# Moving weight loads, token loads and shifted-value loads earlier in a sliding-window attention plus gated feed-forward kernel

## The chip, the cores and the metric

The kernel runs on one core of one Trainium2 chip. The metric is device time in microseconds (us) of one execution. The engines are PE (TensorE, matrix multiplication), PEld (its weight loads), DVE (VectorE), ACT (ScalarE), POOL (GpSimd) and SP (SyncE, which here only issues DMAs). The DMAs that SP issues are in one hardware queue of the page, those that POOL issues in a software queue (when e4, below, gave POOL's 2.78 MB of weight loads to SP, the hardware queue's sum went from 38.48 to 41.26 MB and the software queue's from 13.46 to 10.67). The page counts the packets of both as shares of the same 16 DMA engines (50.8% and 14.2% in the kernel before).

For a kernel on one core, a run is called slow when it is over 1.5% above the fastest run of the same kernel, and fast otherwise. Ratios use fast runs alone.

## The reference, cut to what matters

```python
x  = A_x                                    # 1 x 2048 x 640, bf16
xn = layernorm(x)
# A: 32 heads of 20; a token attends to itself and 7 tokens before it, 2 apart
q, k, v = split(xn @ wqkv)
attn = softmax(q . k[t - 2w], w = 0..7)     # masked where t - 2w < 0
a = (sum_w attn[w] * v[t - 2w]) @ wo
# B: gated feed-forward, no nonlinearity
b = ((xn @ w_gate) * (xn @ w_up)) @ w_down  # 640 -> 1536 -> 640
out = x + a + b
```

## The kernel before: the parts that matter

The 2048 tokens are worked in four chunks of 512. For each chunk, PE makes q, k and v (`psqk`, `psv`), gate and up (`psg`, `psu`) and the output and down projections (`psf`). DVE multiplies q with eight shifted copies of k (the products `pw`); PE sums them per head (`lps`); ACT takes the exponential (`e`). The weights are then stored to memory (`eD`), loaded back transposed (`eT`) and normalised (`rs`), and DVE multiplies them with eight shifted copies of v (`v8`, called `v_606`, `v_729`, `v_855`, `v_929` or only `v` in the profiles) and adds them up. From the second chunk on the normalised tokens `xn` are also stored (`xnD`) and loaded back transposed (`xnT`), for PE to read.

Three pieces of code matter. First, the store and the transposing load of the tokens. The tile `xn` comes from the pool tag `pw`, which has six buffers:

```python
if ttl == 0:
    st["xn"] = apool.tile([P, CH, D], BF, name="xn", tag="pw", bufs=6)
# ...
def keep():
    nc.sync.dma_start(out=xnD[c*CS:(c+1)*CS, :].rearrange(...), in_=st["xn"][:])
    later.append((turn_all, lambda t=clock["dve"]: t + 4.0))
def turn_all():
    nc.sync.dma_start_transpose(out=st["xnT"][:], in_=xnD[...].rearrange(...))
```

Second, the products. They use the same six buffers, so the sixth product after a chunk's `xn` lands in the buffer from which that `xn` is being stored, and waits until the store has landed (4.9 us on the page of the changed kernel, below):

```python
def product(g=g, j=j):
    pt = apool.tile([P, KT, CS], BF, name="pw", tag="pw", bufs=6)
    nc.vector.tensor_tensor(pt[:], st["qT"][:], st["kT"][:, :, off:off+CS], ALU.mult)
```

Third, the loads of the output and down weights, on POOL, and the program's order:

```python
def load_down():
    for jl in range(JL):
        nc.gpsimd.dma_start(out=wo_perm[jl*H:(jl+1)*H, :, :], in_=wo_r[jl])
    nc.gpsimd.dma_start(out=wd[:], in_=B_w_down.rearrange("(f p) d -> p f d", p=P))
# ...
norm(0, 1)
side(load_ffn)                 # gate and up, on POOL
norm(1, 4)
side(constants)
later.append((lambda: load_x(2), when(("turned", 1))))
later.append((load_down, when(("xn", 2, CH - 1))))
weights(0)
side(lambda: want_v8(0))
later.append((lambda: want_v8(1), when(("turned e", 0))))
# ...
```

`side` and `later` feed a small scheduler in the kernel: it simulates PE and DVE while the program is built, and so decides in what order instructions and DMA issues are written.

The softmax here doesn't subtract the row's maximum and nothing guards it: scores larger than these inputs give would overflow.

Of the kernel before, what the change touches and what calls it, by code (L numbers as in the profile page):

```python
# [17 lines left out]
def kernel(  # L18
# [29 lines left out]
    CH = 4  # L48
# [29 lines left out]
    def tcols(ttl):  # L78
        return slice(ttl * P, (ttl + 1) * P)
# [13 lines left out]
    def load_x(c, ttls=range(CH)):  # L93
        for ttl in ttls:
            tg = c * CH + ttl
            x_t = cpool.tile([P, D], BF, name="x_t", bufs=6)
            nc.sync.dma_start(out=x_t[:], in_=x_flat[tg * P : (tg + 1) * P, :])
            x_tiles[tg] = x_t
# [65 lines left out]
    def warm_up(n):  # L164
        wps = ps_log.tile([P, CS], F32, name="wps", tag="lg")
        for k in range(n):
            nc.tensor.matmul(wps[:, 0:P], lhsT=warm[:], rhs=warm[:], start=True, stop=True)
# [5 lines left out]
    clock = {"pe": 5.0, "dve": 2.7, "act": 0.0, "pool": 4.0}  # L173
    main, chain = deque(), deque()
    burst, quick, later = [], [], []
    done = {}
    rings = {"mm": (5, []), "tr": (2, []), "lg": (1, []), "pw": (6, [])}

    def when(*names):
        return lambda: max((done.get(n, INF) for n in names), default=0.0)  # L180

    def on(eng, name, ready, took):
        clock[eng] = max(clock[eng], ready) + took
        done[name] = clock[eng] + LAG

    def op(queue, name, emit, took, need=None, after=None, ring=None, slack=0.0):
        def ready():
            t = need() + slack if need else 0.0
            if ring:
                n, users = rings[ring[0]]  # L190
                if len(users) >= n:
                    t = max(t, done.get(users[-n], INF))
            return t

        queue.append((name, emit, took, ready, after, ring))
# [30 lines left out]
    def norm(c, group):  # L226
        st = state[c]
        st["xnT"] = None

        def alloc():  # L230
            if st["xnT"] is None:
                st["xnT"] = cpool.tile([P, KT, CS], BF, name="xnT", bufs=3)

        def steps(t0):
            g = {}

            def stats():
                g["mv"] = cpool.tile([P, group, nc.vector.BN_AGGR_DIM], F32, name="mv", bufs=2)
                for k in range(group):
                    x_t = x_tiles[c * CH + t0 + k]  # L240
                    s = cpool.tile([P, 2, nc.vector.BN_STATS_DIM], F32, name="stats")
                    for hf in range(2):
                        nc.vector.bn_stats(s[:, hf, :], x_t[:, hf * N2 : (hf + 1) * N2])  # L243
                    nc.vector.bn_aggr(g["mv"][:, k, :], s[:])
                rstd = cpool.tile([P, group], F32, name="rstd", bufs=2)
                g["rstd"] = rstd
                if c == 0 and t0 < 2:
                    nc.scalar.activation(rstd[:], g["mv"][:, :, 1], ACT.Sqrt, bias=eps[:])
                    return
                nc.gpsimd.tensor_scalar(rstd[:], g["mv"][:, :, 1], EPS, None, op0=ALU.add)  # L250
                nc.gpsimd.tensor_tensor(
                    rstd[:], rstd[:], mhalf[:].to_broadcast([P, group]), ALU.pow
                )

            def stats_after(t):
                if c == 0 and t0 < 2:
                    on("act", ("rstd", c, t0), t + LAG, 0.25)
                    return
                on("pool", ("rstd", c, t0), t + LAG, 0.85)

            op(chain, ("stats", c, t0), stats, 1.12 * group, None, stats_after)

            def scaling(ttl, k):
                def scale_x():
                    if c == 0 and t0 < 2:
                        nc.vector.reciprocal(g["rstd"][:], g["rstd"][:])
                    if c < 1:
                        xn_t = apool.tile([P, D], BF, name="xn_t", tag="o16")
                    else:
                        if ttl == 0:  # L270
                            st["xn"] = apool.tile([P, CH, D], BF, name="xn", tag="pw", bufs=6)
                        xn_t = st["xn"][:, ttl, :]
                    nc.vector.tensor_scalar(
                        xn_t[:], x_tiles[c * CH + ttl][:],
                        scalar1=g["mv"][:, k, 0:1], scalar2=g["rstd"][:, k : k + 1],
                        op0=ALU.subtract, op1=ALU.mult,
                    )
                    st["xn", ttl] = xn_t

                def turn():  # L280
                    alloc()
                    pst = ps_tr.tile([P, KT, P], BF, name="pst", tag="tr")
                    for i in range(KT):
                        nc.tensor.transpose(
                            pst[:, i, :], st["xn", ttl][:, i * P : (i + 1) * P], ident[:]
                        )
                    nc.scalar.copy(st["xnT"][:, :, tcols(ttl)], pst[:])
                    if c == ttl == 0:
                        warm_up(14)

                def turned(t):
                    on("act", ("xnT", c, ttl), t + LAG, 0.7)

                def keep():
                    nc.sync.dma_start(
                        out=xnD[c * CS : (c + 1) * CS, :].rearrange("(t p) d -> p t d", p=P),
                        in_=st["xn"][:],
                    )
                    later.append((turn_all, lambda t=clock["dve"]: t + 4.0))

                def turn_all():
                    alloc()
                    nc.sync.dma_start_transpose(
                        out=st["xnT"][:],
                        in_=xnD[c * CS : (c + 1) * CS, :].rearrange("m (k p) -> m k p", p=P),
                    )
                    done["stored", c] = min(clock["pe"], clock["dve"])
                    done["turned", c] = min(clock["pe"], clock["dve"])
                    for k in range(CH):
                        done["xnT", c, k] = done["turned", c] + 8.0  # L310

                def scaled(t):
                    if c >= 1:
                        if ttl == CH - 1:
                            later.append((keep, lambda t=t: t))
                        return
                    op(burst, ("turn", c, ttl), turn, 0.3, when(("xn", c, ttl)), turned,
                       ("tr", ("xnT", c, ttl)), 0.7)

                def later_free():  # L320
                    old = done.get(("turn", c, ttl - 2), INF) if c < 1 else 0.0
                    return max(done.get(("rstd", c, t0), INF), old if ttl >= 2 else 0.0)

                op(chain, ("xn", c, ttl), scale_x, 0.43 if c or t0 >= 2 else 0.53, later_free, scaled,
                   ("pw", ("stored", c)) if c >= 1 and ttl == 0 else None)

            return [lambda k=k: scaling(t0 + k, k) for k in range(group)]

        if group == 1:
            for pair in ((0, 1), (2, 3)):  # L330
                for f in [steps(t0)[0] for t0 in pair]:
                    f()
        else:
            for t0 in range(0, CH, group):
                for f in steps(t0):
                    f()
# [70 lines left out]
    def load_v8(tg):  # L407
        c, ttl = divmod(tg, CH)
        v8 = apool.tile([P, W, D], BF, name="v8")
        rows = vD[tg * P : (tg + 1) * P, :]  # L410
        nc.sync.dma_start(
            out=v8[:],
            in_=bass.AP(tensor=rows.tensor, offset=rows.offset, ap=[[D, P], [DIL * D, W], [1, D]]),
        )
        state[c]["v8", ttl] = v8
        done["v8", tg] = max(done["v", c, ttl, 1] + 2.5, done.get(("add1", tg - 2), 0.0)) + 5.0

    def want_v8(tg):
        if tg < NT:
            c, ttl = divmod(tg, CH)  # L420
            later.append((lambda: load_v8(tg), when(("v", c, ttl, 1))))
# [226 lines left out]
    def side(fn):  # L648
        op(chain, ("side", len(chain)), fn, 0.0)
# [2 lines left out]
    side(load_ffn)  # L652
    norm(1, 4)
    side(constants)
    later.append((lambda: load_x(2), when(("turned", 1))))
    later.append((load_down, when(("xn", 2, CH - 1))))
    weights(0)
    side(lambda: want_v8(0))
    later.append((lambda: want_v8(1), when(("turned e", 0))))
    turned_weights(0)  # L660
    norm(2, 4)
# [62 lines left out]
```

## Time and profile before

| | before |
|---|---|
| time, median of 40 runs | 277.15 us (275.68 to 279.44), all fast |
| span of the profiled run | 275.8 us |
| PE busy | 263.6 us (96%) |
| largest PE wait | 5.4 us, head sums for products of the second chunk |

The first lines are from the page of the kernel before: busy time by engine, then busy tenths in 40 slices of 6.9 us (PEclk is the granted clock in tenths), then the DMA queues with packets, megabytes and share of the 16 engines.

```profile
PE 263.6 (96%) x1607; PEld 145.7 (53%) x1624; DVE 202.7 (74%) x260; ACT 104.1 (38%) x185; POOL 39.0 (14%) x81
...
PE   8899999999998399999999999999999999999994
...
PEclk9999999999999569999999999999999999999999
...
q1 hardware_dynamic: 49920, 38.48, 50.8%
q0 software_dynamic: 3616, 13.46, 14.2%
```

PE is full everywhere except at the start, at the end and in the slice marked 3, and the clock falls just there and after.

The hole, in the timeline of PE of the kernel before (start, time, engine, line, what, count, and in brackets the idle time and what ended it):

```profile
40.94 1.26 PE L442 MATMUL lps<-pw,Ek 128*32 128x512 bf16 x20
...
87.15 1.25 PE L615 MATMUL psf<-wd,hT 128*128 128x320 bf16 x8
91.34 0.58 PE L442 MATMUL lps<-pw,Ek 128*32 128x512 bf16 x1 [2.94 <-DVE pw L431]
92.74 0.58 PE L442 MATMUL lps<-pw,Ek 128*32 128x512 bf16 x1 [0.81 <-DVE pw L431]
94.14 0.59 PE L442 MATMUL lps<-pw,Ek 128*32 128x512 bf16 x1 [0.82 <-DVE pw L431]
95.54 2.29 PE L442 MATMUL lps<-pw,Ek 128*32 128x512 bf16 x17 [0.81 <-DVE pw L431]
97.77 1.51 PE L608 MATMUL psf<-wo_perm,oT 128*128 128x320 bf16 x5
```

The first line is a head sum of the first chunk, which does not wait: all 20 matmuls in 1.26 us. In the second chunk PE waits for four products in turn, and the next matmuls are slow (1.51 us for five that elsewhere take 0.84).

Why the products come so late is told by the chain of waits of the kernel before (start, time, what), followed back from there:

```profile
47.78 0.38 SPq L295
...
48.26 12.24 DMA eT<-eD
...
60.52 1.89 DVE rs L495
...
64.68 2.84 DVE v_606 L510
...
76.48 7.64 DMA v_929<-vD
...
95.54 2.29 PE lps L442 x17
```

The transposing load of the weights takes 12.24 us, and everything on DVE up to the products hangs on it. The next one takes 4.29 us (issued at 108.53, landed at 112.82).

The SP timeline of the kernel before shows the order of issues that the change touches (the second number is how long the issue itself kept SP):

```profile
22.63 0.39 SPq L295 DMA_DIRECT2D xnD<-xn  x1
29.71 2.61 SPq L303 DMA_TRANSPOSE xnT<-xnD  x1
32.38 1.98 SPq L97 DMA_DIRECT2D x_t<-in_A_x_dram  x4
34.46 0.38 SPq L411 DMA_DIRECT2D v_606<-vD  x1
```

Where DMA time was free is read from the windows of the kernel before (window, its length, busy time and count of PE, PEld, DVE, ACT and POOL, granted clock, DMA share, GB/s; the share is the sum of the packets' times over 16 engines, so it can pass 1 where packets overlap):

```profile
25.00:30.00 5.00, 4.95 (x24) 2.25 (x23) 3.66 (x4) 2.57 (x5) 0.00 (x0) 1.00 0.67 249
30.00:35.00 5.00, 5.00 (x37) 2.19 (x38) 4.89 (x6) 2.93 (x5) 0.00 (x0) 1.00 0.85 197
35.00:40.00 5.00, 4.95 (x33) 2.10 (x27) 5.00 (x7) 3.53 (x6) 0.00 (x0) 1.00 0.89 273
40.00:45.00 5.00, 4.95 (x38) 2.06 (x38) 4.20 (x14) 2.85 (x5) 1.28 (x2) 1.00 0.19 68
```

### The profile page before, as it was taken

What the parts mean: (1) busy time and instruction counts of PE and PEld (TensorE: products, weight loads), DVE (VectorE), ACT (ScalarE), POOL (GpSimd) and SP (SyncE); (2) the same over time, 40 slices, a digit from 0 to 9 for tenths busy, and PEclk for the clock granted to TensorE, in tenths of its full rate; (3) what the DMA queues carried; (4) which work ended last, traced back from release to release, by engine and by line L of the source; (5) the groups of instructions that cost most, each with busy time, mean ns of one, the idle gap of its engine ahead of it and who ended that gap; (6) DMA issues with size and microseconds to landing.
All of it is one profiled execution on the core that took longest, in us unless ns stands there. A gap on an engine that the chain in (4) does not pass through costs nothing.

```text
span 275.8 us, 4134 instructions
## 1 busy us (share of the span) xinstructions
PE 263.6 (96%) x1607; PEld 145.7 (53%) x1624; DVE 202.7 (74%) x260; ACT 104.1 (38%) x185; POOL 39.0 (14%) x81
## 2 busy tenths in 40 slices
PE   8899999999998399999999999999999999999994
PEld 8544444446555156744444577744446774445773
DVE  4454997229979997299999975999999989922221
ACT  3655575556554000045555530034552004555000
POOL 1634006001104004000000041130000212000100
PEclk9999999999999569999999999999999999999999
DMA  6999684997797963741860597399169498410111
GB/s 192 304 386 387 157 260 115 322 265 196 234 304 210 321 193 94 208 113 32 274 170 2 178 324 230 125 263 248 38 153 298 112 308 234 127 48 2 48 48 48
DMA packets 53554, 52.18 MB, mean 189 GB/s; under 512 B 24754, under 2 KB 50816, under 8 KB 53536
## 3 DMA queue, kind: packets, MB, share of 16 engines
q1 hardware_dynamic: 49920, 38.48, 50.8%
q0 software_dynamic: 3616, 13.46, 14.2%
q8 instruction: 12, 0.20, 0.3%
q14 instruction: 6, 0.05, 0.1%
HBM read 35.39 MB, written 10.90 MB: 168 GB/s over the span
## 4 chain that ended last, share of the span: by engine, by line
PE 75%; DVE 11%; DMA 10%; SPq 1%; issue 1%; POOL 0%; ACT 0%; ACTq 0%
PE psf L615 19%; PE psu L566 17%; PE psg L566 17%; PE psf L608 8%; PE psqk L359 8%; DMA eT<-eD 4%; PE lps L442 4%; DMA v_929<-vD 3%; PE psv L385 2%; DVE pw L431 2%; DMA vD<-v_t 2%; DMA x_t<-in_A_x_dram 1%; DVE v_929 L510 1%; DVE v_606 L510 1%; DVE v_729 L510 1%
## 5 line engine op out<-in xcount | busy, mean ns | idle before, releaser
L566 PE MATMUL psu<-xnT,wu 128*128 128x512 bf16 x240 | 59.7, 379 | 0.0
L566 PE MATMUL psg<-xnT,wg 128*128 128x512 bf16 x228 | 59.0, 379 | 0.6
L615 PE MATMUL psf<-wd,hT 128*128 128x320 bf16 x384 | 58.2, 302 | 0.0
L571 ACT CAST gs<-psg 128x512 bf16<-128x512 f32 x48 | 28.1, 586 | 70.0 <-PE psg L566 69.1
L431 DVE TENSOR_TENSOR pw<-qT,kT 128x2560 bf16<-128x2560 bf16 x32 | 46.3, 1484 | 3.7 <-ACT kT L365 3.7
L615 PEld LDWEIGHTS <-hT 128*128 128x128 bf16 x384 | 37.9, 99 | 15.3 <-DVE hT L576 0.2
L359 PE MATMUL psqk<-xnT,wqkv 128*128 128x512 bf16 x195 | 43.9, 379 | 0.3
L566 PEld LDWEIGHTS <-wu 128*128 128x128 bf16 x240 | 23.3, 98 | 28.7 <-issue 0.8
L566 PEld LDWEIGHTS <-wg 128*128 128x128 bf16 x240 | 23.3, 98 | 28.2 <-issue 0.8
L571 ACT CAST us<-psu 128x512 bf16<-128x512 f32 x48 | 28.1, 586 | 26.0 <-PE psu L566 26.0
L622 DVE TENSOR_TENSOR osb<-psf,xr 128x320 bf16<-128x320 f32 x32 | 15.4, 488 | 25.9 <-PE psf L615 23.2
L576 DVE TENSOR_TENSOR hT<-gs,us 128x512 bf16<-128x512 bf16 x48 | 19.9, 420 | 17.9 <-ACT us L571 17.6
L359 PEld LDWEIGHTS <-wqkv 128*128 128x128 bf16 x200 | 19.4, 98 | 23.7 <-issue 0.8
L608 PE MATMUL psf<-wo_perm,oT 128*128 128x320 bf16 x160 | 27.6, 304 | 0.0
L385 PE MATMUL psv<-wqkv,xnT 128*128 128x320 bf16 x160 | 22.7, 299 | 0.0
L632 POOL DMA_DIRECT2D out_dram<-osb x13 | 7.1, 547 | 107.9 <-DVE osb L622 107.8
L608 PEld LDWEIGHTS <-oT 128*128 128x128 bf16 x160 | 15.7, 99 | 7.7 <-issue 1.3
L243 DVE BATCH_NORM_STATS2 stats<-x_t 128x6 f32<-128x320 bf16 x32 | 13.6, 467 | 7.4 <-DMA x_t<-in_A_x_dram 7.4
L385 PEld LDWEIGHTS <-xnT 128*128 128x128 bf16 x160 | 15.5, 98 | 6.3
L442 PE MATMUL lps<-pw,Ek 128*32 128x512 bf16 x160 | 13.2, 411 | 5.4 <-DVE pw L431 5.4
L397 POOL DMA_DIRECT2D vD<-v_t x12 | 6.5, 545 | 77.4 <-ACT v_t L391 77.4
L391 ACT CAST v_t<-psv 128x320 bf16<-128x320 f32 x32 | 13.6, 426 | 6.9 <-PE psv L385 6.5
(94 smaller groups left out, 195.7 us busy)
## 6 DMA issues: line engine op xcount, KB each, us to landing
x_t<-in_A_x_dram SPq DMA_DIRECT2D x16, 160.0 KB, 4.8
xr<-in_A_x_dram POOLq DMA_DIRECT2D x16, 160.0 KB, 4.2
out_dram<-osb POOLq DMA_DIRECT2D x13, 160.0 KB, 2.7
wg<-in_B_w_gate_dram POOLq DMA_DIRECT2D x2, 960.0 KB, 10.7
wu<-in_B_w_up_dram POOLq DMA_DIRECT2D x2, 960.0 KB, 12.6
xnD<-xn SPq DMA_DIRECT2D x3, 640.0 KB, 5.3
wd<-in_B_w_down_dram POOLq DMA_DIRECT2D x1, 1920.0 KB, 12.4
vD<-v_t POOLq DMA_DIRECT2D x12, 160.0 KB, 5.4
```

Source lines behind the costliest of these rows:

```text
L243: nc.vector.bn_stats(s[:, hf, :], x_t[:, hf * N2 : (hf + 1) * N2])
L359: nc.tensor.matmul(ps[:], lhsT=wqkv[:, i, r * D + j * P : r * D + (j + 1) * P], rhs=st["xnT"][:, i, :], start=(i == 0), stop=(i == KT - 1),)
L385: nc.tensor.matmul(ps[:, 0:N2], lhsT=st["xnT"][:, i, tcols(ttl)], rhs=wqkv[:, i, 2 * D + n0 : 2 * D + n0 + N2], start=(i == 0), stop=(i == ...
L391: nc.scalar.copy(v_t[:].rearrange("p (j h) -> p j h", j=Dh)[:, :, k * HH : (k + 1) * HH], ps[:, 0:N2].rearrange("p (h j) -> p j h", j=Dh),)
L431: nc.vector.tensor_tensor(pt[:], st["qT"][:], st["kT"][:, :, off : off + CS], ALU.mult)
L442: nc.tensor.matmul(lps[H * j : H * (j + 1), :], lhsT=Ek[:, i, :], rhs=st["pw", g, j][:, i, :], start=(i == 0), stop=(i == KT - 1), tile_po ...
L566: nc.tensor.matmul(ps[:], lhsT=w[:, i, f * P : (f + 1) * P], rhs=st["xnT"][:, i, :], start=(i == 0), stop=(i == KT - 1),)
L571: nc.scalar.copy(s[:], ps[:])
L576: nc.vector.tensor_tensor(h[:], st["gu", 0, f][:], st["gu", 1, f][:], ALU.mult)
L608: nc.tensor.matmul(ps[:, 0:N2], lhsT=st["oT", ttl][:, i, :], rhs=wo_perm[:, i, n0 : n0 + N2], start=(i == 0), stop=False,)
L615: nc.tensor.matmul(ps[:, 0:N2], lhsT=st["hT", f][:, tcols(ttl)], rhs=wd[:, f, n0 : n0 + N2], start=False, stop=(f == FT - 1),)
L622: nc.vector.tensor_tensor(osb[:, n0 : n0 + N2], ps[:, 0:N2], xr[:, n0 : n0 + N2], ALU.add)
```

## The change

The intent is to take the 2.8 MB of output and down weights (wo and wd) out of the time in which eT is loaded, and to put them behind gate and up, where DMA time seemed free. To make room in the hardware queue, the third chunk's tokens and the first shifted values are issued ahead of the second chunk's transposing load.

```diff
                 def keep():
                     nc.sync.dma_start(...)                 # xnD <- xn
+                    done["kept", c] = min(clock["pe"], clock["dve"])
                     later.append((turn_all, lambda t=clock["dve"]: t + 4.0))
 ...
     side(load_ffn)
     norm(1, 4)
     side(constants)
-    later.append((lambda: load_x(2), when(("turned", 1))))
-    later.append((load_down, when(("xn", 2, CH - 1))))
+    side(load_down)
+    later.append((lambda: load_x(2), when(("v", 0, CH - 1, 1))))
+    later.append((lambda: want_v8(0), when(("kept", 1))))
     weights(0)
-    side(lambda: want_v8(0))
     later.append((lambda: want_v8(1), when(("turned e", 0))))
```

The streams of PE, ACT and DVE stay the same, instruction for instruction. Only DMA issues move.

## The prediction

> **What bounds the kernel now.** TensorE: the page gives PE 263.6 of 275.8 us. The PE timeline is gapless except at the start (4 us, untouched) and at 88.4 us, where the second chunk's head sums wait for VectorE's products: 5.4 us in four waits (waits view), the only ones of this kind. The loss is larger: the stretch from 88.4 to 104.4 us holds work that takes 6.4 us at the usual rate (head sums 1.2, output and down matmuls 0.136 each), so 9.7 us go: 7.1 until the fourth product arrives, 2.7 because the granted clock falls to 0.61 and 0.78 in the windows after. [...]
>
> The products are late because the chain of waits runs back through four mix-and-add rounds on VectorE (64.7 to 89.9) and the normalisation (60.5) to the transposing load of the first chunk's weights, eT, which takes 12.24 us (48.26 to 60.50; the others 3.4 to about 5.4). Beside it the queues carry wo and wd (2.8 MB, issued 45.0 to 48.6), the third chunk's store, shifted values v_729 (13.5 us to land, others about 7) and xnT; the DMA share in the windows from 48 to 65 us is 1.0 to 1.18.
>
> **What the change does.** The instruction order shows the streams of TensorE, ScalarE and VectorE unchanged; only DMA issues move. (a) wo and wd go to about 25-29 us on POOL, behind gate and up. (b) The third chunk's x loads go from 32.4 to about 16-22 us, ahead of the second chunk's store. (c) The first shifted values go from 34.5 to about 29 us, ahead of xnT. The windows from 25 to 45 us have DMA shares of 0.67, 0.85, 0.89 and 0.19: about 7 us free, which roughly holds the 2.8 MB (8 us at 350 GB/s, estimated from these windows' rates).
>
> **Gain.** eT's issue is tied to VectorE's third-chunk xn (47.8) and stays near 48.3. Without wd it should take 6 to 7 us, landing near 54.5. The rounds start 6 us earlier; v_729 is there in time; the waits for v_855 and v_929 (1.8, 0.5) stay. The fourth product ends at 89.5 instead of 95.5; PE arrives at 88.4, waits 1.1 us and keeps its clock. Gain 6.0 + 2.5 = 8.5 us, nearly all critical; the rest shifts whole.
>
> **Costs.** The second chunk's store shares the queues with wd and lands perhaps 3 us later (29.7 now); the sixth product reuses its buffer (34.6) and may wait a little; the second head sum has 1.7 us of slack. The second chunk's xnT lands near 45, needed at 54.
>
> **Predicted:** 269.2 us, 8 in 10 between 266.5 and 274.5. Faster by over 2% 0.77, within 2% 0.20, slower 0.03.
>
> **What would show it.** Right: eT lands in 5 to 8 us; lps's wait for pw falls from 5.4 to under 2 us; clock near 1 around 90 us; "rs" starts at 53 to 56; the second chunk's gate matmuls start near 109, not 117. Wrong: eT still needs 10 us (then store, v_729 and xnT congest it, not wd); or the first chunk's products wait for the store near 34 us, giving PE a gap near 35 or 41; or PE waits for gate/up near 26 us.
>
> **What would make it wrong.** The early backlog may run past 45 us, so the eD store at 43.9 queues behind it and eT starts late; or the shifted-value loads, now earlier, meet the vD stores at 67 to 71 us and give back 2 to 3 us.

The 2.5 us suppose that PE keeps its clock at a wait of 1.1 us. That was my estimate, and the text gives no run for it; the trace of the kernel before has a wait of 1.24 us that ends at 10.54 us with the granted clock at 1.00 (8.5 to 11.9 us), and a fall to half at 90.41 us, within a wait of 2.94 us. The 350 GB/s are near what two of the four windows give (249 / 0.67 = 372 and 68 / 0.19 = 358; the other two give 232 and 307). The 6 to 7 us for eT without wd are an estimate; the other three took 3.4 to 5.4 us.

## More of the kernel before

For each DMA the trace holds 16 landing records (2368 for 148 DMAs in the kernel before). Below they are called reports of its 16 engines; that is my reading, since no record names an engine.

The two queue lines give the mean packet: 38.48 MB / 49920 = 771 bytes in the hardware queue, and 13.46 MB / 3616 = 3720 bytes in the software queue.

## The result, and the profile after

A ratio is the mean time of one kernel's fast runs over that of the other's in the same rounds, so it is not quite the ratio of the medians quoted.

| | before | changed |
|---|---|---|
| median, all runs | 277.15 us (40 runs) | 275.56 us (20 runs) |
| lowest to highest | 275.68 to 279.44 | 270.43 to 280.76 |
| runs called slow | 0 of 40 | 13 of 20 |
| ratio of fast runs | | 0.9832 (0.98 to 0.9865) |

The fast runs are 1.7% faster and their mean, 272.6 us, lies in the predicted range; the gain is under the 2% that I thought likely. Most striking is the spread, 10.3 us from the lowest to the highest against 3.8 us in the kernel before. The range holds only by the fast runs: the median of all 20, 275.56 us, lies above it. If one counts all 20 runs, the mean is 275.43 us, and only 0.7% is gained over the 277.27 us of before.

The profile that came with these runs is of a slow one (277.1 us). I ran the changed kernel again later, for a fast one (273.19 us, span 271.3); its expectation is quoted among the experiments as run e5. Both show the same thing, so it is not something that only slow runs show. First the page of the slow one: PE, clock, and the group of the products (busy time, mean ns, idle time before them and what ended most of it).

```profile
PE   7899996999999799999999999999999999999994
...
PEclk9999997999999979999999999999999999999999
...
L432 DVE TENSOR_TENSOR pw<-qT,kT 128x2560 bf16<-128x2560 bf16 x32 | 46.4, 1485 | 8.6 <-DMA xnD<-xn 4.9
```

There is a new hole in the seventh slice, and the products now wait 4.9 us for the store of the second chunk's tokens. In the fast run, the chain of waits over 20 to 65 us says it in three lines:

```profile
22.57 16.46 DMA xnD<-xn
...
40.95 2.82 DVE pw L432 x2
...
43.81 1.24 PE lps L443 x17
```

The store took 16.46 us to land, against 7.0 us before (22.63 to 29.65). The PE timeline of the same fast run, at the new hole and at the old one:

```profile
41.10 0.39 PE L443 MATMUL lps<-pw,Ek 128*32 128x512 bf16 x2
42.41 0.38 PE L443 MATMUL lps<-pw,Ek 128*32 128x512 bf16 x1 [0.91 <-DVE pw L432]
43.81 1.24 PE L443 MATMUL lps<-pw,Ek 128*32 128x512 bf16 x17 [1.03 <-DVE pw L432]
...
92.25 0.38 PE L443 MATMUL lps<-pw,Ek 128*32 128x512 bf16 x1 [0.69 <-DVE pw L432]
93.65 1.24 PE L443 MATMUL lps<-pw,Ek 128*32 128x512 bf16 x17 [1.02 <-DVE pw L432]
```

Both holes are there: the old one much smaller (1.7 us instead of 5.4, and no slow matmuls after it), the new one 1.9 us. The windows of the fast run that answer to those of before:

```profile
25.00:30.00 5.00, 4.95 (x24) 2.25 (x23) 3.50 (x4) 2.73 (x5) 3.36 (x5) 1.00 1.06 375
30.00:35.00 5.00, 5.00 (x33) 2.18 (x35) 4.70 (x5) 2.77 (x5) 0.00 (x0) 1.00 1.03 268
35.00:40.00 5.00, 4.95 (x36) 2.15 (x26) 0.88 (x1) 3.68 (x6) 0.00 (x0) 1.00 1.02 364
40.00:45.00 5.00, 3.06 (x27) 0.99 (x26) 4.96 (x8) 1.17 (x2) 0.00 (x0) 1.00 1.32 243
```

The DMA share is over 1 from 25 to 45 us: the free time is used up. DVE works 0.88 us in the third window, where it worked 5.00 before, and PE 3.06 us in the fourth, where it worked 4.95.

The whole difference can be laid out by three starts on PE, read from the timelines and the trace:

| us | before | changed, slow run | changed, fast run (e5) | with a separate buffer (e1, below) |
|---|---|---|---|---|
| second chunk's q and k start | 54.02 | 58.87 | 56.86 | 53.82 |
| second chunk's gate starts | 117.18 | 116.61 | 112.84 | 109.73 |
| between the two | 63.16 | 57.74 | 55.98 | 55.91 |
| from there to the end | 158.6 | 158.6 | 158.4 | 158.4 |

Between the two starts the change gains 7.2 us in the fast run (63.16 - 55.98). Before them it loses 2.8 us (56.86 - 54.02). After them nothing differs.

The slow run loses two more pieces of nearly the same size: 2.0 us before the first start and 1.8 us between the two. The trace's clock record has two stretches of 3.41 us at half the clock, at 44.9 and 96.1 us, right after the two holes, and the fast run has none there. Half of 3.41 us is 1.7 us of lost work each time, by estimate. By the trace's busy times, PE was busy for 33% and 46% of the 3.41 us just before these two stretches. But for the last stretch of each record, which the record's end cuts off, the stretches of two clock records are whole multiples of 3.413 us: 12, 1, 14, 1 and 52 times in the slow run (40.96, 3.41, 47.79, 3.41 and 177.49 us), and 25, 3 and 51 times in the kernel before (85.33, 10.24 and 174.08 us). So I took the record to run in windows of that length. Laid through the fast run, where no fall marks them, they are an estimate: the first hole then lies partly in one window (56% busy) and partly in the next (86%), the second in a window that is 50% busy, and the clock stayed. That the place of a wait in these windows decides whether a run is slow is my reading of these two runs; it was not tested.

### The profile page after: what moved, and what is told of

Read it like the earlier page. It is cut to its first block, busy times and chain, and to the rows that moved or that the text cites. A ratio compares the mean times of both kernels' runs of the same rounds, so it can differ in the third digit from the quotient of the medians.

```text
span 275.2 us, 4138 instructions
## 1 busy us (share of the span) xinstructions
PE 263.7 (96%) x1607; PEld 145.2 (53%) x1624; DVE 202.4 (74%) x260; ACT 104.1 (38%) x185; POOL 39.2 (14%) x81
## 3 DMA queue, kind: packets, MB, share of 16 engines
q0 software_dynamic: 3616, 13.46, 14.0%
## 4 chain that ended last, share of the span: by engine, by line
PE 69%; DVE 13%; DMA 12%; SPq 2%; issue 2%; POOL 0%; ACT 0%; DVEq 0%; ACTq 0%
PE psf L616 19%; PE psu L567 17%; PE psg L567 16%; PE psf L609 8%; DMA xnD<-xn 6%; PE psqk L360 4%; PE lps L443 4%; DMA v_929<-vD 3%; DMA x_t<-in_A_x_dram 3%; DVE pw L432 3%; PE psv L386 2%; SPq L107 2%; DVE stats L243 1%; DVE v_929 L511 1%; DVE v_407 L511 1%
## 5 line engine op out<-in xcount | busy, mean ns | idle before, releaser
L567 PE MATMUL psu<-xnT,wu 128*128 128x512 bf16 x240 | 60.7, 384 | 0.0
L360 PE MATMUL psqk<-xnT,wqkv 128*128 128x512 bf16 x195 | 43.9, 379 | 0.3
```

Of the source, the lines that this page charges most:

```text
L360: nc.tensor.matmul(ps[:], lhsT=wqkv[:, i, r * D + j * P : r * D + (j + 1) * P], rhs=st["xnT"][:, i, :], start=(i == 0), stop=(i == KT - 1),)
L567: nc.tensor.matmul(ps[:], lhsT=w[:, i, f * P : (f + 1) * P], rhs=st["xnT"][:, i, :], start=(i == 0), stop=(i == KT - 1),)
```

## The experiments

**My theory (A):** the move of wo and wd does what I said, but the DMA time it takes away belongs to the store of the second chunk's tokens. The store shares the 16 engines with wd, which lies in the other queue; it lands late; the sixth product, which reuses its buffer, waits; DVE, then PE, then the weights' store eD and eT start late. **Rival (B):** the third chunk's token loads, put ahead of the store in the same queue, delay it. **Rival (C):** the total DMA backlog makes eT late whatever the order, or the spread is a state of the chip and has nothing to do with the store.

Twelve runs were made (e1 to e4 on one chip, e5 to e12 on another).

### e1: a separate buffer for the second chunk's tokens

A try with one more buffer did not build, so the tile borrows one of the two buffers of the shifted values, which is idle at that time. All instructions and DMA issues stay in place.

```diff
-    st["xn"] = apool.tile([P, CH, D], BF, name="xn", tag="pw", bufs=6)
+    if c == 1:
+        st["xn"] = apool.tile([P, W, D], BF, name="xn", tag="v8")[:, 0:CH, :]
+    else:
+        st["xn"] = apool.tile([P, CH, D], BF, name="xn", tag="pw", bufs=6)
```

> The changed kernel, but the second chunk's normalised tokens lie in a buffer of the shifted-value pool, so the sixth product of the first chunk no longer waits for their store; every instruction and DMA issue stays in place. Theory (the change is right but the store of the second chunk, 16.8 us to land, holds the sixth product by 4.9 us and so takes back about 4.9 us plus 2 us of clock): store still lands late (33 to 40 us), no wait of a product for it, no PE gap at 41 us, eT lands before 55 us, time 268 to 270 us, and the spread of the runs shrinks from 10 us to about 3. Rival (the late eT or the shifted values congest in any case): PE still loses 5 us or more near 90 us and the time stays at 273 to 277.

Measured: 270.29 us (269.93 to 270.65, six runs, all fast), ratio 0.974 (0.9709 to 0.9772), against 277.43 us. The store landed at 36.6 us, late as expected, and no product waited for it. eT landed at 52.46 us, 4.2 us after its issue. The PE timeline of e1 has no hole at 41 us (first line), and this is what is left near 90 us:

```profile
40.74 1.26 PE L446 MATMUL lps<-pw,Ek 128*32 128x512 bf16 x20
...
88.13 0.39 PE L446 MATMUL lps<-pw,Ek 128*32 128x512 bf16 x2
89.14 0.38 PE L446 MATMUL lps<-pw,Ek 128*32 128x512 bf16 x1 [0.62 <-DVE pw L435]
90.54 1.24 PE L446 MATMUL lps<-pw,Ek 128*32 128x512 bf16 x17 [1.03 <-DVE pw L435]
```

So the wait for the buffer is what took the gain back, and with it went most of the spread (0.7 us in these six runs; 3.4 us in e9, the same kernel again). Rival C falls. The DVE timeline of e1 shows two terms that I had wrong by about a microsecond each:

```profile
54.69 0.42 DVE L580 TENSOR_TENSOR hT<-gs,us 128x512 bf16<-128x512 bf16 x1 [1.64 <-ACT us L575]
55.03 1.87 DVE L499 TENSOR_REDUCE rs<-eT 128x128 f32<-128x1024 bf16 x1
...
73.50 2.83 DVE L514 TENSOR_TENSOR v<-v,eT 128x5120 bf16<-128x5120 bf16 x1 [2.93 <-DMA v<-vD]
```

`rs` starts at 55.03 although eT had landed at 52.46: in DVE's stream it stands behind the first chunk's last gate product `hT`, which waits for ACT. And the wait for the third shifted values is 2.93 us, where it was 1.81 before.

### e2: only the weight loads early

wo and wd early; tokens and shifted values as before.

```diff
-    later.append((lambda: load_x(2), when(("v", 0, CH - 1, 1))))
-    later.append((lambda: want_v8(0), when(("kept", 1))))
+    later.append((lambda: load_x(2), when(("turned", 1))))
     weights(0)
+    side(lambda: want_v8(0))
```

> Only the early wo and wd loads; third chunk's x loads and the first shifted values as before. Theory A (the wd load in the other queue, whose packets are 5120 bytes against 1280, starves the last engines of the store): the store still lands late, 32 us or more, in most runs, PE gap at 41 us, time like the changed kernel, 272 to 277 with a wide spread. Theory B (the x loads put ahead of the store delay it): store lands by 32 us, no gap at 41, time 269 to 271.

Measured: 275.45 us (270.13 to 276.10); five of six runs slow by the rule, so there is no ratio, and the profile is of a slow one. It fits neither expectation, and the one fast run (270.13 us) was not profiled. In the slow one, the store landed at 29.73 us, early; but the third chunk's tokens, which now stand behind the second chunk's transposing load, landed at 44.86 us instead of 38.45, and DVE waited 4.1 us for them. That transposing load had kept SP for 10.2 us (2.61 before). Theory A as I had stated it was too narrow: not the store as such is the victim, but what stands in the hardware queue while wd is in the software queue.

### e3: everything but the weight loads

```diff
-    side(load_down)
+    later.append((load_down, when(("xn", 2, CH - 1))))
     later.append((lambda: load_x(2), when(("v", 0, CH - 1, 1))))
```

> Only the early x loads and early shifted values; wo and wd late as before. Theory A: store lands by 31 us, no wait for it, but eT again takes 10 us or more beside wd, PE waits about 5 us at 88 us, time 276 to 278. Theory B: store lands after 33 us and the sixth product waits.

Measured: 277.21 us (four runs), ratio 1.0002 (0.9946 to 1.0058). The store landed at 31.8 us, 2.1 us later than before; no product waited; eT took 11.96 us again. Token loads ahead of the store cost it 2 us, not 10, so rival B alone falls. Theory A alone has not passed either: e2 moved wd without the tokens, and the store was early. The late store needs both, as the table below shows. Without moving wd nothing is gained.

### e4: the weight loads in the hardware queue, behind the store

```diff
-    side(load_down)
+    later.append((load_down, when(("kept", 1))))
     later.append((lambda: want_v8(0), when(("kept", 1))))
```

In `load_down`, `nc.gpsimd` becomes `nc.sync`.

> The changed kernel, but wo and wd are issued on the same hardware queue as the store, right behind it[...]. Theory A: store lands at 29 to 32 us with all 16 engines close together, no wait of a product, no PE gap at 41, wd lands by about 42, eT in under 8 us, time 268 to 270, spread about 3 us. Theory B (total DMA backlog, not the queue, is what delays): the store or eD is late again, and time is above 272.

Measured: 270.45 us (269.81 to 272.77), ratio 0.9758 (0.9718 to 0.9798). The buffer is shared as in the changed kernel, yet no product waits: the store landed at 33.9 us (15 of 16 engines by 31.32). wd landed at 42.7 us and eT in 3.4 us. The same bytes at nearly the same time, in the store's own queue and behind it, do no harm. The queue is not all that changed. The DMA queues on the page of e4, to be compared with those of the kernel before:

```profile
q1 hardware_dynamic: 52176, 41.26, 58.4%
q0 software_dynamic: 2960, 10.67, 11.1%
```

The hardware queue has 2.78 MB more in 2256 more packets; by the trace's list of packets, wo and wd went in packets of 1280 bytes here and of 5120 (some of wo's of 2560) in the software queue. So e4 changes the queue, the order and the packet size together, and does not say which of the three helps. One expectation missed: the engines were not all close together, since one lagged by 2.6 us.

### e5: the changed kernel again

> The changed kernel itself, on the same chip and rounds as the next three, to see whether its spread (270.4 to 280.8 us over 20 runs) comes back and what a run looks like in another draw. Theory (a draw decides when the last of the 16 engines finishes the store of the second chunk): runs spread over 5 us or more; in a run below 272.5 us the store lands by about 35 us and no product waits for it, in a run above 275 us it lands later than 37 us and the sixth product waits. Rival (the spread is the chip's state, independent of the store): the store's landing does not go with the time.

Measured: 274.59 us (273.19 to 279.60), ratio 0.9899 (0.9847 to 0.9951). The spread came back (6.4 us). My guess of what sets a fast run apart found no support, though the profiled run lies between my two marks: in a run of 273.19 us the store landed at 39.03 us and the sixth product waited 4.3 us, as in the slow one. What differed was the clock. The granted mean clock of the 26 runs in which the changed kernel was timed sorts them well (the windows in brackets are an estimate, explained below the table):

| mean granted clock | runs | mean time, us |
|---|---|---|
| 0.998 to 1.000 (none halved) | 10 | 272.9 |
| 0.991 to 0.994 (about one window) | 9 | 276.0 |
| 0.988 to 0.985 (two) | 5 | 277.7 |
| 0.982 and 0.980 (three) | 2 | 280.2 |

One window of 3.41 us at half the clock lowers the mean of a 275 us run by 3.41 / 2 / 275 = 0.006; the profiled slow run has two such windows and a mean of 0.988. Part of the time between the rows is the waits themselves, which also differ. No run of the changed kernel under 272.5 us was profiled, so whether the store lands early in those stays open.

### e6: separate buffer, token loads late

The kernel of e1, with `load_x(2)` back at `when(("turned", 1))`.

> As the run with the separate buffer, but the third chunk's x loads stay where they were before, behind the transposing load of the second chunk. Theory (moving wd up takes the DMA time of whatever stands last in the other queue; the x loads then land late, statistics on VectorE wait and the weights' store eD and eT follow): x lands after 42 us, VectorE waits 3 to 5 us for it, eD issued at 47 to 49 instead of 45.7, PE waits 3 to 4 us near 90, time 273 to 276. Rival (moving x up was not needed): time 270 to 271.

Measured: 277.24 us (four fast runs), ratio 0.9994 (0.9951 to 1.0038). The whole gain is gone, more than I expected. The SP timeline of e6 shows why:

```profile
30.72 13.46 SPq L307 DMA_TRANSPOSE xnT<-xnD  x1
44.24 1.99 SPq L97 DMA_DIRECT2D x_t<-in_A_x_dram  x4
51.83 0.40 SPq L475 DMA_DIRECT2D eD<-e  x1
```

The transposing load, issued beside wd, kept SP for 13.46 us (2.61 before), so the tokens could not even be issued before 44.24. They landed at 49.09. DVE's wait for them, in the waits of e6 from 20 to 100 us (total, times, longest):

```profile
DVE stats L243 <- DMA x_t<-in_A_x_dram: 7.6, 1, 7.6
```

eT was then issued at 55.46 and landed at 60.67, the time at which it had landed before (60.49). So the early token loads are not an extra: with the shifted values early, moving wd without the tokens is worth nothing. (In e2, where the shifted values were late as well, SP was kept for 10.2 us and eT landed at 57.41 us; its runs lay between 270.13 and 276.10 us.)

### e7: separate buffer, first shifted values late

The kernel of e1, with `side(lambda: want_v8(0))` back behind `weights(0)`.

> As the run with the separate buffer, but the first shifted values stay behind the transposing load of the second chunk. Theory: they are not needed before eT (52 us), so nothing changes, 270 to 271 us. Rival (the early shifted values matter): they land after 57 us or hold up eD, time above 272.

Measured: 272.54 us (270.50 to 276.70), ratio of fast runs 0.9786 (0.975 to 0.9822); two of six runs slow, among them the profiled one. By the fast runs it cannot be told from the separate buffer alone (0.979 in e9, same chip), but the median lies above the 270 to 271 us of my theory, and the profiled run does what the rival said. In the profiled run, the shifted values were issued at 45.39, right ahead of the small store eD (46.00), which then took 7.2 us to land instead of 2.5 in e1. I leave open how often that happens. Of the runs with the early shifted values, the early tokens and the separate buffer, e1, e8, e9 and e11 had no slow one in 24, and e12 had one in six.

### e8: separate buffer, and both head sums of the second chunk later

PE's stream is changed so that one more group of output and down matmuls stands ahead of each of the second chunk's two head sums. The edit is the slack that the kernel's scheduler adds for head sums; it reorders parts of DVE's and ACT's streams too.

```diff
-    ("lg", ("exp", c, g)), 0.7)
+    ("lg", ("exp", c, g)), 3.5 if c == 1 else 0.7)
```

> As the run with the separate buffer, plus one more group of output and down matmuls (about 2.9 us of PE work) ahead of the second chunk's first head sums, to fill the rest of the PE wait at 88 us (1.6 us of waits, 2.0 us lost). Theory: wait of head sums for products under 0.3 us, time 268 to 269. Rival (later stages take it back, as products or stores end later): 270 or more.

Measured: 274.93 us (273.64 to 276.67), ratio 0.9896 (0.9863 to 0.9929). A miss: the second chunk's gate did start 1.9 us earlier than in e1 (107.83), but the rest took 164.7 us instead of 158.4. The edit reordered the third chunk as well, and PE then waited there for transposed outputs (1.8 us), for products (1.8) and for ACT (1.2).

### e9: the separate buffer again

> The changed kernel with the separate buffer again, in the same rounds as the next three. Theory: 270 to 271 us on any chip, spread about 1 to 2 us, no halved clock window near 42 us. Rival (the first such run was a lucky draw): 272 or more and a spread of 4 us or more.

Measured: 271.09 us (269.85 to 273.25, all fast), ratio 0.9791 (0.9749 to 0.9832), on the other chip. The store landed at 41.64 us, and nothing waited for it. Three of the six runs have a mean clock of 0.994; the profiled run has no hole at 41 us but 2.1 us of waits near 90. By the estimate under e5, 0.994 is one window at half the clock; no profile shows where it lies. The spread of 3.4 us is more than the 1 to 2 us that I expected.

### e10: control, the kernel before with the separate buffer

> Control: the kernel before with only the separate buffer. Theory (the buffer matters only where the store is late; before, it lands at 29.7 and the sixth product comes at 34.6): same as before, ratio 0.995 to 1.005. Rival (the buffer helps of itself): 2 us or more faster.

Measured: 277.23 us, ratio 1.001 (0.9969 to 1.0051). The buffer alone does nothing; it matters only where the store is late.

### e11: both cures

> Separate buffer, and wo and wd on the hardware queue behind the store. Theory: the store and the third chunk's x no longer share engines with the 5120 byte packets of wd, so the last engine of the store is done by 34 us; but nothing waits for it any more, so the time is that of the separate buffer alone within 0.5 us. Rival (the last engine's delay still costs elsewhere): faster by 1 us or more.

Measured: 271.02 us (270.07 to 272.34), ratio 0.9783 (0.9749 to 0.9818), the same as e9 in the same rounds. The store's last engine was done at 31.91 us instead of 41.64, and it bought nothing, as theory A has it: here the late store cost only through what waited for it.

### e12: separate buffer, only the first head sums later

```diff
-    ("lg", ("exp", c, g)), 0.7)
+    ("lg", ("exp", c, g)), 3.5 if (c, g) == (1, 0) else 0.7)
```

> Separate buffer, and only the first head sums of the second chunk moved behind one more group of output and down matmuls (the earlier try moved both head sums and lost in later stages). Theory: wait of 1.6 us near 88 us gone, order on the DMA queue unchanged, 268 to 269.5 us. Rival (any such move loses later, as products of the third chunk come late again): 271 or more.

Measured: 269.63 us (268.26 to 273.14, one of six slow), ratio 0.9725 (0.9682 to 0.9768). The first head sums no longer wait, the second now wait 1.0 us at 98.76. The median lies just above the forecast of 268 to 269.5 us. It is the lowest median and 2.7% faster than before, although its interval overlaps that of e9.

### When the store of the second chunk's tokens landed, in all profiles

The table is from the trace's records of DMA landings: the store's issue, when the 12th, the 15th and the last of the 16 engines had reported, and where wo and wd were. The last engine is the one that counts here: in e5 the 15th had reported at 38.03 us and the last at 39.03, and the product that waited started at 39.12.

| kernel | wo, wd | tokens of chunk 3 | issued | 12th | 15th | last |
|---|---|---|---|---|---|---|
| before | late | behind | 22.63 | 29.27 | 29.57 | 29.65 |
| e10 | late | behind | 23.17 | 28.96 | 29.97 | 30.80 |
| e3 | late | ahead | 22.65 | 30.79 | 31.71 | 31.80 |
| e2 | early, other queue | behind | 22.50 | 29.41 | 29.53 | 29.73 |
| e6 | early, other queue | behind | 22.88 | 29.07 | 29.66 | 29.99 |
| changed (slow run) | early, other queue | ahead | 22.61 | 29.95 | 33.97 | 39.40 |
| e5 | early, other queue | ahead | 22.57 | 34.80 | 38.03 | 39.03 |
| e1 | early, other queue | ahead | 25.06 | 30.44 | 31.86 | 36.60 |
| e7 | early, other queue | ahead | 23.10 | 30.95 | 35.38 | 42.52 |
| e8 | early, other queue | ahead | 22.64 | 34.67 | 36.25 | 41.84 |
| e9 | early, other queue | ahead | 22.99 | 32.05 | 35.02 | 41.64 |
| e12 | early, other queue | ahead | 22.51 | 30.63 | 38.20 | 39.20 |
| e4 | early, same queue | ahead | 25.41 | 30.82 | 31.32 | 33.90 |
| e11 | early, same queue | ahead | 22.55 | 31.15 | 31.47 | 31.91 |

It takes both halves. With wd in the other queue but no tokens ahead, the store is through by 29.99 us, early in the transfer of wo and wd (in e2, 117 of their 576 packets had begun when it landed). With tokens ahead but wd late, it is at 31.80. With both, the last engines need until 36.6 to 42.5 us in seven profiles of seven, while in five of these seven twelve engines were done by 32.05. With both, but wd in the store's own queue, it is 31.9 and 33.9.

Why the other queue hurts so much was not shown; what the trace's list of packets shows is sizes and counts. wd's packets in the software queue are 5120 bytes, four rows; the store's packets in the hardware queue are 1280 bytes, one row. That packets of the two queues take turns, so that about four bytes of wd move for each byte of the store (5120 / 1280), is my estimate from the counts that follow, not a measurement. In e9, from 36 to 39 us, the hardware queue began 170 packets of 1280 bytes and the software queue 167 of 5120. In e7, in the same stretch, one engine alone still had the store to finish: the hardware queue began 12 packets, and the software queue 199, which would be 12.4 for each of the 16 engines if they were spread evenly. In the changed kernel's slow run, from 36 to 39 us, it was 207 of 1280 and 158 of 5120. The slow eT of the kernel before fits as well: from 53 to 57 us the hardware queue began 241 packets of 256 bytes, of transposing loads, and the software queue 276 of 5120, about 23 bytes of wd for each of theirs. No run was made to test the turns by packet size alone: e4 and e11, which put wd into packets of 1280 bytes, changed the queue and the order with it. Nor is it shown why a few engines lag: the packed trace does not name the engine of a packet.

## Why the prediction was right or wrong, point by point

- **What bounds the kernel, and why the products were late: right.** Without wd beside it, eT took 3.4 to 4.6 us in e1, e4, e9 and in both profiles of the changed kernel, instead of 12.24 (predicted 6 to 7). With wd back (e3), it took 11.96.
- **"Gain 6.0 + 2.5 = 8.5 us": right in kind, 1.3 us too large.** The issue of eT, which I had at 48.3, slipped to 52.12 and 53.11 us in the changed kernel, since the products came late; it goes with the loss before the first start of the table. Between the two starts of the table it was 7.2 us, in the fast run and in e1. In e1 the fourth product came at 90.54 instead of the predicted 89.5: `rs` started at 55.03 instead of 54.5, because it stands behind the last gate product; the wait for the third shifted values grew by 1.1 us; the wait of 0.5 us for the fourth went away.
- **"lands perhaps 3 us later (29.7 now); the sixth product reuses its buffer (34.6) and may wait a little": the step that failed, by its size.** The coupling was named, and so was the gap near 41 us as a sign of error. But the store landed 9.4 and 9.8 us later in the changed kernel's two profiles, not 3, and the product waited 4.3 and 4.9 us. I had reckoned with the queues' mean rate, as if the store got its share of the engines evenly. What counted was the last of 16 engines (in e5 the product started 0.09 us after its report), and the packets beside it were four times as large (5120 bytes against 1280). With the "1.7 us of slack" used up, PE lost 2.8 us at 41 us in the fast run, and 4.9 us in the slow one with its halved clock window.
- **"about 7 us free, which roughly holds the 2.8 MB": right as a sum, misleading as an argument.** The DMA share rose over 1 from 25 to 45 us, and everything did land by about 48. But in this full stretch the store, for which a compute engine waits, took 16.46 us to land in e5 instead of 7.0 before, and in e2 and e6 it was the tokens, not the store, that came late (44.86 and 49.09 us, against 38.45 before). In e4 and e11, with wd behind the store in the same queue, no product waited for the store, and DVE's longest wait for the tokens was 0.8 us (e4).
- **"so the eD store at 43.9 queues behind it and eT starts late": not so in the changed kernel** (eD took 2.1 us in both of its profiles; it was issued late because DVE was late), but this is what e7's profile shows.
- **The forecast time: the range held, the class did not.** The fast runs' mean is 272.6 us, within 266.5 to 274.5 but well above 269.2; the ratio of 0.9832 is a gain of 1.7%, where I gave "faster by over 2%" a chance of 0.77. With the one wait removed (e1), the same change gives 270.29 us and 2.6%. The wide spread I had not foreseen at all. That the range held is in part luck: it was wide enough for a loss of 2.8 us that the forecast does not contain, and the median of all runs lies outside it. Of the signs that I had named (fast and slow run), eT's time came out even shorter than 5 to 8 us (4.18 and 4.59). Not met were the waits of head sums for products (3.6 and 4.2 us, not under 2), the start of `rs` (58.08 and 60.09, not 53 to 56) and the start of the second chunk's gate (112.84 and 116.61, not near 109). The clock held near 90 us in the fast run and fell at 96.1 in the slow one. The gap near 41 us, a sign of error, came.

## What to carry to other kernels

When you move a large load into free DMA time, list what else is in the queues then and which instruction waits for each, down to buffers shared through a pool; a store that nobody seems to need is needed by the next user of its buffer. Judge such a transfer by the landing of its last engine and not by the mean bandwidth (in e9 the 15th of 16 had reported at 35.02 us, the last at 41.64), and put a bulk load behind the urgent transfers in the same queue (here the store then landed at 31.9 and 33.9 us instead of 36.6 to 42.5), or give the urgent one's buffer to someone who needs it later. If a change widens the spread of the times, look at the granted clock of each run: short waits of PE can cost a halved window on top (in the slow run, 1.8 us of waits near 94 us were followed by 3.41 us at half the clock). Here, removing the wait gave back most of the steadiness along with the time.

## What the traces also show of the queues and the clock

- The same load of wd, with rows of 1280 bytes, went in packets of one row in the hardware queue (e4, e11) and of four rows, 5120 bytes, in the software queue. The hardware store with tokens ahead and that software load beside it landed at 36.6 to 42.5 us, and at 31.9 to 33.9 with the same load in its own queue.
- Issuing the transposing load of the tokens kept SP, and so the DMAs that it issues later, for 2.61 us in the kernel before at 29.7 us, and for 11.14 us (the next one of the same kernel, at 53.15 us), 13.46 us (e6) and 11.21 us (e4, wd in the same queue) beside the load of wd.
- The clock was halved for one window of 3.41 us after 1.8 us of waiting, in two pieces with matmuls between (changed kernel, slow run, at 96.1 us), and not after 1.7 us in the fast run. In the kernel before it fell at 90.41 us, 2.0 us after PE had gone idle at 88.40, at the end of a window in which PE was busy for 41%. In the 14 profiles, leaving out the last 10 us of each, it fell after all eight windows at full clock in which PE was busy for 46% or less, and after none with 48% or more; in the last 10 us two windows with 44% passed without a fall (one in the slow run of the changed kernel, at 270.2 us), so these counts give no sharp limit.
